# An attention and experts kernel on one core: preparation of a pair issued a unit later on ScalarE, hash factors on VectorE, the finish of a pair in smaller parts

## The chip, the cores and the metric

The kernel runs on one core of a Trainium2 chip. The metric is the device time of one execution in microseconds (us). TensorE (PE) multiplies matrices, VectorE (DVE), ScalarE (ACT) and GpSimd (POOL) work element by element, SyncE (SP) only issues transfers. Each engine takes its instructions in program order and waits on semaphores of the others.

## The reference

Three stages follow each other; the change touches the first alone, the attention. Queries and keys are hashed to 6 bits, and only those with the same hash attend to each other:

```python
q_bits = (np.einsum('bhsd,dk->bhsk', q, proj) > 0).astype(np.int64)
k_bits = (np.einsum('bhsd,dk->bhsk', k, proj) > 0).astype(np.int64)
q_bucket = np.sum(q_bits * powers, axis=-1)      # powers = 2 ** np.arange(6)
k_bucket = np.sum(k_bits * powers, axis=-1)
mask = q_bucket[:, :, :, None] == k_bucket[:, :, None, :]
scores = scale * np.matmul(q, k.transpose(0, 1, 3, 2))
scores = np.where(mask, scores, -1000000000.0)
scores = scores - np.max(scores, axis=-1, keepdims=True)
attn = np.exp(scores)
attn = attn / (np.sum(attn, axis=-1, keepdims=True) + 1e-09)
return np.matmul(attn, v)
```

There are 2 batches of 8 heads, 768 tokens, 64 numbers a head. The result, 1536 rows of 512, goes through gated products (`a * b @ w_out` with 1536 hidden columns) and then to one of 8 experts for each row.

## The kernel before

**Pairs and units.** Heads are taken in 8 pairs `i`; a pair fills the 128 partitions with two heads of 64. A head has six blocks of 128 queries, and a *unit* `u` is two of them, so a pair has six units and the attention has 48: `u = 6 i + r`. Tile `(u, t)` is block `t` (0 or 1) of unit `u`. The loop over `u` writes the whole order by hand; no scheduler moves anything.

**A tile's way.** `scores` (L170, L172, PE) multiplies queries and keys, and adds the product of the hash signs (`qf`, `kf`), which is zero for equal hashes and hugely negative otherwise; the buffer `st` in PSUM has two copies, so the scores of tile n+2 wait until the exponential has read tile n. `rowmax` (L177, DVE) takes the row maximum `nm`, `expo` (L183, ACT) the exponential `e` and its sum, `recip` (L187, DVE) and `normal` (L192 to L196, POOL) scale it, `turn` (L203, DVE) transposes it, and `pv` (L212, PE) multiplies it by `v`, four units behind: half a head in each unit with `u % 3` of 0 and 1. In the units with `u % 3 == 2` the `epilogue` (L230, ACT) copies the product out of the PSUM banks `pvb` and frees them.

**Preparing a pair.** Every sixth unit (1, 5, 11, 17, 23, 29, 35) `turned` transposes the raw queries and keys of a coming pair on PE into the banks `pvb` (L107), and ACT copies them to `k` and `q` (L121); four transfers on SP's queue make the swapped copies `ks` and `qs`, and `load` fetches the raw data of the pair after. Three units later (3, 8, 14, 20, 26, 32, 38) `signs` multiplies them by the hash projection (L145, L139, PE, into `pvb`), ACT takes the signs `sk` and `qf` (L150, L140), and two multiplications by `self.fac` make `kf` (L152, POOL; DVE for the first pair). These closures (`out`) run at the end of the same unit, behind `expo(u, 1)`.

**Finishing a pair.** `finish_add` (L234, POOL) adds the two halves of the product in three column groups of 256, `finish_high` (L238, ACT) casts the sum to `xh`, `finish_low` (L242, POOL) subtracts to get the rest `xl`. They run in the units with remainder 0 to 3 of the next but one pair.

**What else stands in the order.** `hook(u, at)` puts the conversion of the first weights of the gated products into the units, step by step (L396 to L424, on DVE, POOL and ACT), and in units 41, 44 and 47 the first gated products (L493, PE, into `pvb`) with their ACT copies L501 and L506.

Of the kernel before, what the change touches and what calls it, by code (L numbers as in the profile page):

```python
# [13 lines left out]
AF = mybir.ActivationFunctionType  # L14
ALU = mybir.AluOpType
# [6 lines left out]
def f32(ap):  # L22
    return ap.bitcast(F32)


class Kernel:
# [37 lines left out]
    def attention(self, xh, xl, pools, hook):  # L64
        nc = self.nc
        sb, ps_s, ps_pv = pools
        NB = self.proj.shape[1]
        S, D = self.S, self.D
        NC = S // 128
        pairs = [(b, hp) for b in range(self.B) for hp in range(self.H // 2)]  # L70

        NB32 = S // 32
        H2 = S // 2
# [6 lines left out]
        raw, Q, QS, K, KS, QF, KF, VR = {}, {}, {}, {}, {}, {}, {}, {}  # L80

        def load(i, qs=(nc.sync, nc.sync)):
            b, hp = pairs[i]
            t = raw[i] = sb.tile([128, 2, NC, 2, D], F32, tag="raw", name="raw", bufs=1)
            for j in range(2):
                for n, src in ((1, self.k), (0, self.q)):
                    qs[n].dma_start(out=t[:, n, :, j, :], in_=src[b, 2 * hp + j].rearrange("(p c) d -> p c d", c=NC))

        def load_v(h):
            (b, hp), j = pairs[h // 2], h % 2  # L90
            t = VR[h] = sb.tile([128, 4, NC * D], F32, tag="vr", name="vr", bufs=2)
            src = self.v[b, 2 * hp + j].rearrange("(a r c) d -> r a (c d)", a=4, c=NC)
            for a in range(4):
                nc.sync.dma_start(out=t[32 * a:32 * a + 32], in_=src)

        def halves(t):
            return t.rearrange("p (a b) -> p a b", a=2)
# [6 lines left out]
        def turned(i, n):  # L104
# [25 lines left out]

            return out

        def signs(i, n):
            p = pvb[:, 2 * n:2 * n + 2]
            lz = self.lz.rearrange("p a b c -> p (a b c)")
            if n == 0:
                QF[i] = sb.tile([128, S], BF16, tag="qf", name="qf", bufs=2)
                for x in range(2):
                    nc.tensor.matmul(p[:, x, :H2], lz, Q[i][:, x * H2:(x + 1) * H2], start=True, stop=True)  # L139
                return lambda: nc.scalar.activation(halves(QF[i]), p[:, :, :H2], AF.Sign, bias=self.bias, scale=2.0 ** 100)  # L140
            KF[i] = sb.tile([128, 2, H2], BF16, tag="kf", name="kf", bufs=2)
            sk = sb.tile([128, H2], BF16, tag="sk", name="sk", bufs=1)
            for x in range(2):
                r = slice(64 * x, 64 * x + 64)
                nc.tensor.matmul(  # L145
                    p[r, 0, :H2], lz[:, r], K[i][:, x * H2:(x + 1) * H2], start=True, stop=True, tile_position=(0, 64 * x)
                )

            def out(eng=nc.gpsimd):
                nc.scalar.activation(sk, p[:, 0, :H2], AF.Sign, bias=self.bias, scale=2.0 ** 100)  # L150
                for j in range(2):
                    eng.tensor_scalar(KF[i][:, j], sk, self.fac[:, j:j + 1], None, ALU.mult)  # L152

            return out

# [3 lines left out]
        def small(tag):  # L159
            return sb.tile([128, 2], F32, tag=tag, name=tag, bufs=4)  # L160

        def scores(u, t):
            i, j, g = units[u]
            c = 2 * g + t
            st = ST[u, t] = ps_s.tile([128, 2, 512], F32, tag="s", name="st")
            ql = slice(c * 128, (c + 1) * 128)
            rows = [slice(64 * n, 64 * n + 64) for n in range(2)]
            for n, d in enumerate(rows):
                q, k = (Q[i], K[i][:, n * H2:(n + 1) * H2]) if n == j else (QS[i], KS[i])
                nc.tensor.matmul(st[:, n, :H2], q[d, ql], k[d], start=True, stop=False, tile_position=(64 * n, 0))  # L170
            for n, d in enumerate(rows):
                nc.tensor.matmul(st[:, n, :H2], QF[i][d, ql], KF[i][d, j], start=False, stop=True, tile_position=(64 * n, 0))  # L172

        def rowmax(u, t):
            if t == 0:
                NM[u] = small("nm")
            nc.vector.tensor_reduce(NM[u][:, t:t + 1], ST[u, t][:, :, :H2], axis=AX.XY, op=ALU.max, negate=True)  # L177

        def expo(u, t):
            if t == 0:  # L180
                SU[u] = small("su")
            e = E[u, t] = sb.tile([128, 2, H2], F32, tag="e", name="e", bufs=6)
            nc.scalar.activation(e, ST.pop((u, t))[:, :, :H2], AF.Exp, bias=NM[u][:, t:t + 1], accum_out=SU[u][:, t:t + 1])  # L183
# [14 lines left out]
        def turn(u, t):  # L198
            i, j, g = units[u]
            h, c = 2 * i + j, 2 * g + t  # L200
            if c == 0:
                ET[h] = sb.tile([128, NB32, NC, 32], F32, tag="et", name="et", bufs=2)
            nc.vector.transpose(ET[h][:, :, c], E.pop((u, t)).rearrange("p a (b s) -> p (a b) s", s=32))  # L203
# [25 lines left out]
        def epilogue(h, n):  # L229
            nc.scalar.copy(place(h // 2, n, h % 2, every), product(n, every))  # L230

        def finish_add(i, col, rows=slice(0, 128), eng=nc.gpsimd):
            x, y = (t[rows, col] for t in XP[i])
            eng.tensor_tensor(x, x, y, ALU.add)  # L234

        def finish_high(i, col):
            b, hp = pairs[i]
            nc.scalar.copy(xh[b][:, hp, col], XP[i][0][:, col])  # L238

        def finish_low(i, col, eng=nc.gpsimd):  # L240
            b, hp = pairs[i]
            eng.tensor_tensor(xl[b][:, hp, col], XP[i][0][:, col], f32(xh[b][:, hp, col]), ALU.subtract)  # L242

        NU = len(units)
        cols = [slice(256 * g, 256 * g + 256) for g in range(3)]
# [13 lines left out]
        hook(-1, 0)  # L259
        load_v(0)  # L260
        load_v(1)
        signs(0, 1)(nc.vector)
        signs(0, 0)()
        scores(0, 0)

        for u in range(NU + 2):
            i, r = divmod(u, 6)
            s, w = u % 3, u - 2
            act, last, tr = u < NU, 0 <= u - 1 < NU, w >= 0
            done, fin = divmod(u - 11, 6) if u >= 11 else (-1, 0)  # L270
            preps, new = [], len(pairs)
            if u == 1 or s == 2 and r == 5:
                new = 1 if u == 1 else (u + 7) // 6
                kind = turned
            elif u == 3 or s == 2 and u > 2:
                new = 1 if u == 3 else i + 1
                kind = signs
            if act:
                rowmax(u, 0)
                scores(u, 1)  # L280
                expo(u, 0)
            if s == 2 and u >= 8:
                for n in range(2):
                    epilogue((u - 8) // 3, n)
            if u + 1 < NU:
                scores(u + 1, 0)
            if last:
                recip(u - 1)
                normal(u - 1)
            if tr:  # L290
                turn(w, 0)
            hook(u, 3)
            if act:
                rowmax(u, 1)
            if tr:
                turn(w, 1)
            if new < len(pairs):
                preps = [kind(new, x) for x in (1, 0)]
            elif s < 2 and u >= 6:
                pv((u - 6) // 3, range(12 * s, 12 * s + 12))  # L300
            hook(u, 0)
            if act:
                expo(u, 1)
            for prep in preps:
                prep(*((nc.scalar,) if kind is turned else ()))
            if preps and kind is turned and new + 1 < len(pairs):
                load(new + 1)
            if s == 1 and u >= 7 and (u - 1) // 3 < 2 * len(pairs):
                load_v((u - 1) // 3)
            hook(u, 1)  # L310
            if done == len(pairs) - 2:
                for g in range(3):
                    if fin == 1:
                        finish_add(done, cols[g])
                    if fin == 2:
                        finish_high(done, cols[g])
                        finish_low(done, cols[g])
            elif 0 <= done:
                if fin in (1, 2):
                    for g in ((0, 1), (2,))[fin - 1]:  # L320
                        finish_add(done, cols[g])
                if fin == 3:
                    finish_high(done, slice(0, S))
                if fin in (3, 4):
                    for g in ((0, 1), (2,))[fin - 3]:
                        finish_low(done, cols[g])
            hook(u, 4)
        end = len(pairs) - 1
        for n in range(2):
# [874 lines left out]
```

## Time and profile before

| what | us |
|---|---|
| median of three runs | 781.94 (781.47 to 782.32) |
| the profiled execution | 781.45 |
| its span, first to last instruction | 779.7 |
| PE busy in the span | 720.6 |
| POOL busy | 457.6 |
| DVE busy | 463.6 |
| ACT busy | 342.4 |
| attention, from the start to the last probability product | about 271 |

The rows below are read as follows. A row of the timeline has its start and its length, then engine, line, operation, written and read tiles with their shapes; in brackets the idle time of the engine ahead of it and who ended that. `x4` are four instructions merged. A row by windows has the stretch, its length, and the busy time of PE, PE's weight loads, DVE, ACT and POOL with their instruction counts, then the granted clock of PE as a share of 2.4 GHz, the busy share of the DMA engines and GB/s.

### The profile page before, as it was taken

The numbers are of one execution on the slowest core, as the hardware profiler recorded it, in microseconds if no ns is written. First come the engines' busy times: TensorE is split into PE (matmuls) and PEld (weight loads), VectorE is DVE, ScalarE is ACT, GpSimd is POOL, SyncE is SP. The second block draws the span as 40 slices with busy tenths as digits, with TensorE's granted clock in tenths as the row PEclk, the third lists the DMA queues.
The fourth block names the chain that finished last, engine by engine and source line by source line (L and its number), as shares of the span: only waits on it lengthen the run. The fifth ranks groups of instructions, "written<-read, shape, count | busy, mean of one in ns | idle before, by whom it ended". The sixth has DMA issues, their size and how long they took to land.

```text
span 779.7 us, 16454 instructions
## 1 busy us (share of the span) xinstructions
PE 720.6 (92%) x6832; PEld 599.8 (77%) x6832; DVE 463.6 (59%) x681; ACT 342.4 (44%) x597; POOL 457.6 (59%) x466
## 2 busy tenths in 40 slices
PE   6788888887887899999999999999999999999996
PEld 4345445454554789999999999999998898899995
DVE  3788787686777355364564555623754765556551
ACT  3566566566555434322212121223353755564651
POOL 0678879788787537356363562654441765565651
PEclk9999999999999999999999999999999999999999
DMA  6845273352313403113121130163252576675520
GB/s 151 166 114 117 67 178 77 80 146 55 95 43 89 131 1 110 53 59 105 31 78 55 55 108 3 51 216 107 87 160 91 175 232 235 213 247 202 211 76 22
DMA packets 67485, 87.62 MB, mean 112 GB/s; under 512 B 28739, under 2 KB 40003, under 8 KB 67408
## 3 DMA queue, kind: packets, MB, share of 16 engines
q1 hardware_dynamic: 63200, 78.81, 34.9%
q0 software_dynamic: 2560, 7.34, 2.5%
q8 instruction: 54, 0.88, 0.5%
q10 hardware_dynamic: 1648, 0.39, 0.3%
q14 instruction: 23, 0.19, 0.1%
HBM read 75.52 MB, written 7.34 MB: 106 GB/s over the span
## 4 chain that ended last, share of the span: by engine, by line
PE 78%; ACT 8%; DVE 5%; issue 4%; POOL 3%; DMA 1%; SPq 0%; POOLq 0%; ACTq 0%; DVEq 0%
PE ab L493 22%; PE yp L519 12%; PE op L836 10%; PE hp L786 9%; PE pv L212 8%; PE st L170 5%; ACT e L183 3%; DVE nm L177 2%; PE pv L139 2%; PE hr L804 2%; PE part L493 1%; PE lgp L602 1%; DVE et L203 1%; ACT co L230 1%; PE pv L493 1%
## 5 line engine op out<-in xcount | busy, mean ns | idle before, releaser
L493 PE MATMUL ab<-xh,w 128*128 128x384 f32 x704 | 185.7, 338 | 0.0
L493 PEld LDWEIGHTS ab<-xh,w 128*128 128x128 f32 x704 | 127.7, 188 | 0.8
L507 POOL TENSOR_TENSOR g<-a,g 128x384 fp32r<-128x384 f32 x48 | 54.8, 1141 | 114.5 <-ACT g L506 105.1
L183 ACT ACTIVATE e<-st,nm 128x768 f32<-128x768 f32 x96 | 86.5, 904 | 76.2 <-DVE nm L177 37.7
L493 PE MATMUL ab<-xl,w 128*128 128x384 f32 x352 | 118.3, 336 | 0.0
L177 DVE TENSOR_REDUCE nm<-st 128x1 f32<-128x768 f32 x96 | 90.5, 944 | 39.7 <-PE st L172 39.5
L742 POOL TENSOR_TENSOR w<-raw,w 128x1024 fp32r<-128x1024 f32 x36 | 88.1, 2450 | 36.8 <-ACT w L741 35.8
L170 PE MATMUL st<-ks,qs 64*128 64x384 f32 x192 | 86.3, 530 | 20.8 <-ACT e L183 20.8
L519 PE MATMUL yp<-w,g 128*128 128x512 f32 x432 | 103.4, 391 | 1.0 <-DVE a L505 0.7
L170 PE MATMUL st<-k,q 64*128 64x384 f32 x192 | 86.5, 531 | 14.8 <-ACT e L183 14.7
L196 POOL TENSOR_SCALAR e<-e,s,mc 128x768 f32<-128x768 f32 x96 | 96.1, 1008 | 5.3
L203 DVE STREAM_TRANSPOSE et<-e 128x768 f32<-128x768 f32 x96 | 92.5, 965 | 11.2 <-POOL e L196 9.3
L519 PEld LDWEIGHTS yp<-w,g 128*128 128x128 f32 x432 | 80.3, 188 | 16.7 <-DVE a L505 1.0
L836 PE MATMUL op<-w,hth 128*128 128x512 f32 x256 | 81.7, 400 | 0.0
L212 PE MATMUL pv<-et,vr 32*64 32x192 f32 x3072 | 79.4, 354 | 2.0 <-issue 1.5
L212 PEld LDWEIGHTS pv<-et,vr 32*64 32x64 f32 x3072 | 66.2, 145 | 19.5 <-issue 14.4
L786 PE MATMUL hp<-xgh,w 128*128 128x256 f32 x448 | 80.6, 281 | 0.0
L506 ACT CAST g<-a 128x384 fp32r<-128x384 f32 x48 | 24.8, 516 | 110.4 <-DVE a L505 110.4
L742 DVE TENSOR_TENSOR w<-raw,w 128x1024 fp32r<-128x1024 f32 x28 | 64.6, 2307 | 14.5 <-ACT w L741 14.5
L786 PEld LDWEIGHTS hp<-xgh,w 128*128 128x128 f32 x448 | 69.1, 188 | 0.3
L741 ACT CAST w<-raw 128x1024 fp32r<-128x1024 f32 x64 | 66.2, 1045 | 3.5 <-PE yp L519 3.5
L493 PEld LDWEIGHTS ab<-xl,w 128*128 128x128 f32 x352 | 66.2, 188 | 0.8
(190 smaller groups left out, 1183.8 us busy)
## 6 DMA issues: line engine op xcount, KB each, us to landing
raw<-in_moe_w_dram SPq DMA_DIRECT2D x32, 1024.0 KB, 5.3
vr<-in_v_dram SPq DMA_DIRECT2D x64, 192.0 KB, 3.9
raw<-in_moe_w_a_dram SPq DMA_DIRECT2D x5, 1024.0 KB, 5.0
raw<-in_moe_w_b_dram SPq DMA_DIRECT2D x5, 1024.0 KB, 5.3
raw<-in_moe_w_out_dram SPq DMA_DIRECT2D x5, 1024.0 KB, 5.0
raw<-in_k_dram SPq DMA_DIRECT2D x16, 192.0 KB, 4.9
qs<-q SPq DMA_DIRECT2D x16, 192.0 KB, 3.1
ybuf<-y SPq DMA_DIRECT2D x12, 256.0 KB, 6.3
```

The source lines that it names most:

```text
L170: nc.tensor.matmul(st[:, n, :H2], q[d, ql], k[d], start=True, stop=False, tile_position=(64 * n, 0))
L177: nc.vector.tensor_reduce(NM[u][:, t:t + 1], ST[u, t][:, :, :H2], axis=AX.XY, op=ALU.max, negate=True)
L183: nc.scalar.activation(e, ST.pop((u, t))[:, :, :H2], AF.Exp, bias=NM[u][:, t:t + 1], accum_out=SU[u][:, t:t + 1])
L196: nc.gpsimd.tensor_scalar(E[u, t], E[u, t], r[:, t:t + 1], c[:, t:t + 1], ALU.mult, ALU.add)
L203: nc.vector.transpose(ET[h][:, :, c], E.pop((u, t)).rearrange("p a (b s) -> p (a b) s", s=32))
L212: nc.tensor.matmul(pvb[m:m + 64, a, :NC * 32], v[d], et[d, n].rearrange("p c s -> p (c s)"), start=(n < 2), stop=(n >= NB32 - 2), tile_pos ...
L493: nc.tensor.matmul(p[:, :384], w[:, k, fs], x[:, k, cols], start=(k == 0 and n == 0), stop=(k == self.KD - 1 and n == 2),)
L519: nc.tensor.matmul(p, g[:, f, rows], w[:, f], start=(n == 0), stop=(n == 5))
L741: nc.scalar.copy(h, raw)
L742: eng.tensor_tensor(l, raw, f32(h), ALU.subtract)
L786: nc.tensor.matmul(p[:, :256], w[:, k, fs], x[:, k], start=(n == 0), stop=(n == 3 * self.KD - 1))
L836: nc.tensor.matmul(p, h[:, 2 * n + f, rows], w[:, f], start=(n == 0 and f == 0 and m == 0), stop=(n == 3 and f == 1 and m == 2),)
```

## The change

1. The closures of `turned` and `signs` are kept in `preps` and run in the next unit, behind that unit's first exponential `expo(u, 0)`; so do the copies' transfers and the `load` behind them. PE's part (transposes, sign products) stays where it was, now after `expo(u, 1)` in the text of the loop.
2. `expo(u, 1)` stands before `hook(u, 0)`, so before the ACT copies of the first gated products.
3. The two multiplications that make `kf` are put off into `later` and run on VectorE (`masks`), behind the second transposition of the unit in which ACT takes the signs.
4. The finish of a pair is a table: the cast `xh` in two parts of 512 and 256 columns, one unit apart from the additions and subtractions, over units with remainder 0 to 4. The last two pairs keep their own finish.

```diff
+        later = []
+        def masks():
+            for kf, sk in later:
+                for j in range(2):
+                    nc.vector.tensor_scalar(kf[:, j], sk, self.fac[:, j:j + 1], None, ALU.mult)
+            later.clear()
...
-            def out(eng=nc.gpsimd):
+            def out(*_):
                 nc.scalar.activation(sk, p[:, 0, :H2], AF.Sign, bias=self.bias, scale=2.0 ** 100)
-                for j in range(2):
-                    eng.tensor_scalar(KF[i][:, j], sk, self.fac[:, j:j + 1], None, ALU.mult)
+                later.append((KF[i], sk))
...
+        finish = (
+            (1, finish_add, (cols[0],)), (1, finish_add, (cols[1],)), (2, finish_add, (cols[2],)),
+            (2, finish_high, (slice(0, 512),)), (3, finish_low, (cols[0],)),
+            (4, finish_high, (cols[2],)), (4, finish_low, (cols[1],)), (5, finish_low, (cols[2],)),
+        )
...
             if act:
                 rowmax(u, 0)
                 scores(u, 1)
                 expo(u, 0)
+            for prep in preps:
+                prep(nc.scalar)
+            if preps and kind is turned and held + 1 < len(pairs):
+                load(held + 1)
+            preps = []
...
             if tr:
                 turn(w, 1)
+            masks()
+            if act:
+                expo(u, 1)
...
             if new < len(pairs):
-                preps = [kind(new, x) for x in (1, 0)]
+                preps, held = [kind(new, x) for x in (1, 0)], new
...
             hook(u, 0)
-            if act:
-                expo(u, 1)
-            for prep in preps:
-                prep(*((nc.scalar,) if kind is turned else ()))
-            if preps and kind is turned and new + 1 < len(pairs):
-                load(new + 1)
...
-                if fin == 3:
-                    finish_high(done, slice(0, S))
+                for start, step, args in finish:
+                    done, fin = divmod(u - 11 - start, 6)
+                    if fin == 0 and 0 <= done < len(pairs) - 2:
+                        step(done, *args)
```

What this does to the order is seen best at unit 26, where the signs of a pair are prepared. On ACT, from the epilogue of unit 26 on (`xp`, `co`), before:

```order
L230 COPY xp_2398<-pv_127 64x4x6x32
L230 COPY co_2399<-pv_127 64x4x6x32
L183 ACTIVATE e_2428,su_2395<-st_2390,nm_2388 128x768
L150 ACTIVATE sk_2422<-pv_127,bias_84 128x384
L140 ACTIVATE qf_2425<-pv_127,bias_84 128x768
L238 CAST xh0_98<-xp_1956 128x768
L183 ACTIVATE e_2445,su_2444<-st_2402,nm_2437 128x768
L183 ACTIVATE e_2513,su_2444<-st_2439,nm_2437 128x768
```

and after the change (line numbers are those of the changed file, the numbers of the tiles differ):

```order
L237 COPY xp_2402<-pv_127 64x4x6x32
L237 COPY co_2403<-pv_127 64x4x6x32
L190 ACTIVATE e_2425,su_2399<-st_2394,nm_2392 128x768
L190 ACTIVATE e_2443,su_2442<-st_2406,nm_2435 128x768
L158 ACTIVATE sk_2428<-pv_127,bias_84 128x384
L148 ACTIVATE qf_2431<-pv_127,bias_84 128x768
L190 ACTIVATE e_2467,su_2442<-st_2437,nm_2435 128x768
L245 CAST xh0_98<-xp_1959 128x256
```

The first exponential of unit 27 now stands ahead of the signs, the second behind them, and only the last part of the cast is left here, behind both.

On DVE, in unit 27 and at the start of unit 28, before:

```order
L177 TENSOR_REDUCE nm_2437<-st_2402 128x1
L187 RECIPROCAL r_2452<-su_2395 128x2
L203 STREAM_TRANSPOSE et_2417<-e_2312 128x24x32
L177 TENSOR_REDUCE nm_2437<-st_2439 128x1
L203 STREAM_TRANSPOSE et_2417<-e_2380 128x24x32
L177 TENSOR_REDUCE nm_2516<-st_2447 128x1
```

and after:

```order
L184 TENSOR_REDUCE nm_2435<-st_2406 128x1
L194 RECIPROCAL r_2452<-su_2399 128x2
L210 STREAM_TRANSPOSE et_2421<-e_2315 128x24x32
L184 TENSOR_REDUCE nm_2435<-st_2437 128x1
L210 STREAM_TRANSPOSE et_2421<-e_2335 128x24x32
L138 TENSOR_SCALAR kf_2427<-sk_2428,fac_86 128x384 x2
L184 TENSOR_REDUCE nm_2519<-st_2447 128x1
```

The two multiplications for `kf` come in between the second transposition of unit 27 and the first row maximum of unit 28. On POOL they stood between two units' `normal`, and are gone there. The order on SP's queue is the same before and after.

## Rows read from the trace of the kernel before

**Rows 1.** The page's slices of 19.5 us each: PE's busy tenths.

```profile
PE   6788888887887899999999999999999999999996
```

**Rows 2.** Windows from one pair's transposes to the next; the last ends at products.

```profile
38.22:67.52 29.30, 24.55 (x478) 14.66 (x477) 25.36 (x37) 18.13 (x34) 22.84 (x37) 1.00 0.36 86
67.52:98.77 31.25, 26.02 (x476) 15.76 (x477) 23.57 (x33) 19.22 (x36) 25.52 (x41) 0.95 0.48 117
98.77:129.49 30.72, 26.02 (x476) 15.76 (x476) 23.60 (x34) 19.23 (x36) 24.36 (x39) 0.94 0.48 115
129.49:160.50 31.01, 26.03 (x477) 15.61 (x477) 23.46 (x34) 19.32 (x36) 24.82 (x39) 0.94 0.41 94
160.50:190.85 30.35, 25.94 (x476) 15.80 (x476) 22.62 (x32) 18.63 (x34) 25.14 (x41) 0.94 0.40 97
190.85:221.67 30.82, 26.07 (x476) 16.11 (x476) 24.39 (x34) 18.18 (x34) 24.06 (x40) 0.94 0.38 98
```

**Rows 3.** Timeline of PE in units 24 to 27: scores and sign products.

```profile
133.53 0.59 PE L170 MATMUL st<-k,q 64*128 64x384 f32 x1 [1.48 <-ACT e L183]
...
143.70 0.87 PE L145 MATMUL pv<-k,lz 128*64 128x384 f32 x4 [0.41 <-ACT co L230]
...
145.99 0.59 PE L170 MATMUL st<-ks,qs 64*128 64x384 f32 x1
...
149.14 0.59 PE L170 MATMUL st<-ks,qs 64*128 64x384 f32 x1 [2.07 <-ACT e L183]
```

**Rows 4.** Windows of two `pv` runs and of unit 45's scores with their `pv`.

```profile
134.54:136.67 2.13, 2.13 (x98) 1.85 (x96) 1.91 (x3) 0.97 (x2) 1.77 (x6) 1.00 0.91 221
...
150.44:153.89 3.45, 3.45 (x98) 2.79 (x97) 2.01 (x3) 2.12 (x4) 3.08 (x7) 0.60 0.02 5
...
242.21:246.82 4.61, 4.61 (x103) 2.91 (x103) 3.56 (x6) 1.99 (x4) 4.17 (x8) 0.66 0.02 5
```

**Rows 5.** Timeline of ACT in units 23 to 27: copies, signs, cast, exponentials.

```profile
131.08 0.81 ACT L121 ACTIVATE k<-pv 128x768 f32<-128x768 f32 x1 [0.60 <-PE pv L107]
...
132.48 0.91 ACT L183 ACTIVATE e<-st,nm 128x768 f32<-128x768 f32 x1
...
142.85 0.80 ACT L230 COPY co<-pv 64x768 f32<-64x768 f32 x1
...
146.09 0.58 ACT L150 ACTIVATE sk<-pv,bias 128x384 bf16<-128x384 f32 x1 [1.43 <-PE pv L139]
...
147.36 0.83 ACT L238 CAST xh<-xp 128x768 fp32r<-128x768 f32 x1
148.08 0.91 ACT L183 ACTIVATE e<-st,nm 128x768 f32<-128x768 f32 x1
```

**Rows 6.** Timeline of DVE: the first row maxima of units 24 and 27.

```profile
130.32 0.95 DVE L177 TENSOR_REDUCE nm<-st 128x1 f32<-128x768 f32 x1
...
143.97 0.95 DVE L177 TENSOR_REDUCE nm<-st 128x1 f32<-128x768 f32 x1
```

**Rows 7.** Line L152: count, then ns min/median/max, first and last start (us).

```profile
L152 POOL TENSOR_SCALAR kf<-sk,fac x14: 1247/1253/1261, 32.3 to 208.8; 128x384 bf16<-128x384 bf16 x14
L152 DVE TENSOR_SCALAR kf<-sk,fac x2: 313/316/320, 11.8 to 12.0; 128x384 bf16<-128x384 bf16 x2
```

**Rows 8.** Timeline around unit 44: DVE's row maximum, ACT's cast, PE's scores.

```profile
238.90 0.95 DVE L177 TENSOR_REDUCE nm<-st 128x1 f32<-128x768 f32 x1
...
239.01 0.51 ACT L506 CAST g<-a 128x384 fp32r<-128x384 f32 x1 [3.12 <-DVE a L505]
...
240.59 0.59 PE L170 MATMUL st<-ks,qs 64*128 64x384 f32 x1 [2.28 <-ACT e L183]
```

**Rows 9.** Timeline: a conversion step on DVE twice, and POOL's `normal`.

```profile
38.81 2.12 POOL L196 TENSOR_SCALAR e<-e,s,mc 128x768 f32<-128x768 f32 x2
...
39.47 0.60 DVE L404 TENSOR_SCALAR r<-spare 128x512 int32<-128x512 uint32 x1
...
143.67 0.39 DVE L404 TENSOR_SCALAR r<-spare 128x512 int32<-128x512 uint32 x1
```

More of the change, by code (lines that the diff above doesn't have):

```diff
@@ L139, in signs @@
                     nc.tensor.matmul(p[:, x, :H2], lz, Q[i][:, x * H2:(x + 1) * H2], start=True, stop=True)
-                return lambda: nc.scalar.activation(halves(QF[i]), p[:, :, :H2], AF.Sign, bias=self.bias, scale=2.0 ** 100)
+                return lambda *_: nc.scalar.activation(halves(QF[i]), p[:, :, :H2], AF.Sign, bias=self.bias, scale=2.0 ** 100)
             KF[i] = sb.tile([128, 2, H2], BF16, tag="kf", name="kf", bufs=2)
@@ L261, in attention @@
         load_v(1)
-        signs(0, 1)(nc.vector)
+        signs(0, 1)()
+        masks()
         signs(0, 0)()
         scores(0, 0)
+        preps = []
[4 more added lines that the diff above has]
+        )
         for u in range(NU + 2):
@@ L270, in attention @@
             done, fin = divmod(u - 11, 6) if u >= 11 else (-1, 0)
[L271 to L277, printed above, removed]
+            new = len(pairs)
             if act:
@@ L281, in attention @@
                 expo(u, 0)
+            for prep in preps:
+                prep(nc.scalar)
+            if preps and kind is turned and held + 1 < len(pairs):
+                load(held + 1)
+            preps = []
             if s == 2 and u >= 8:
@@ L296, in attention @@
                 turn(w, 1)
+            masks()
+            if act:
+                expo(u, 1)
+            if u == 1 or s == 2 and r == 5:
+                new, kind = 1 if u == 1 else (u + 7) // 6, turned
+            elif u == 3 or s == 2 and u > 2:
+                new, kind = 1 if u == 3 else i + 1, signs
             if new < len(pairs):
-                preps = [kind(new, x) for x in (1, 0)]
+                preps, held = [kind(new, x) for x in (1, 0)], new
             elif s < 2 and u >= 6:
@@ L317, in attention @@
                         finish_low(done, cols[g])
[L318 to L321, printed above, removed]
-                if fin == 3:
-                    finish_high(done, slice(0, S))
-                if fin in (3, 4):
-                    for g in ((0, 1), (2,))[fin - 3]:
-                        finish_low(done, cols[g])
+            else:
+                for start, step, args in finish:
+                    done, fin = divmod(u - 11 - start, 6)
+                    if fin == 0 and 0 <= done < len(pairs) - 2:
+                        step(done, *args)
             hook(u, 4)
```

## Prediction, written before the changed kernel ran

> **What bounds the kernel now.** I read the page's slices first: from the fifteenth on (273 us), where the gated products have begun, PE is busy for 90% or more; before that, in the attention, mostly for 70 to 90% [rows 1]. So there is something to win in the attention alone. Then I cut the attention at the transposes of each pair [rows 2]: one pair of heads takes 29.3 to 31.3 us, and PE, the busiest engine, has work for 24.6 to 26.1 of it. So the change is worth what it takes out of the first 260 us, and each us there is a us of the whole, because PE works in order.
>
> The timeline of PE inside one pair shows where its 5 us of idling are. It runs gapless through the units with probability products, and stops at the unit that prepares another pair: 1.48 us before the scores at 133.53 and 2.07 us before those at 149.14, both times until an exponential on ACT [rows 3]. Why the exponential is late stands in ACT's timeline: the two copies k and q (131.08), or the two signs (146.09) and a cast of the finished pair (147.36), are queued ahead of it [rows 5]. Its row maximum had been ready long before: DVE starts the maximum for the 148.08 exponential at 143.97 [rows 6]. And the second stop costs more than itself: the 96 products after it take 3.45 us at a granted clock of 0.60, a mix of 1.2 and 2.4 GHz, where the same 96 took 2.13 us at 1.00 [rows 4].
>
> **The change, part by part: one pair walked through.** I take the pair of units 24 to 29 (129.49 to 160.50, 31.01 us), with the durations of the rows, and move what moves. A row maximum takes 0.95 and a hand-over of 0.1; from an exponential's start to the scores that need its buffer are 1.05 (132.48 to 133.53) [rows 3, 5].
>
> *Copies k and q a unit later.* DVE's maximum at 130.32 is untouched [rows 6], so the exponential starts at 130.32 + 1.05 = 131.37 instead of 132.48, the scores at 132.42 instead of 133.53. The copies follow: 131.37 + 0.89, then 1.40 for both (131.08 to 132.48), then 0.15 to the end and over to PE: 133.8. The probability products write the banks that q is read from, so they start there and not at 133.4 when the scores are through: a new wait of 0.4. Now they start at 134.54 [rows 4]. Gain 0.72. Everything up to the sign products (143.70) is PE after PE or hangs on it, and moves with it: 142.98.
>
> *Signs a unit later, the cast out of their way.* The sign products take 2.29 (143.70 to 145.99) and end at 145.27. The maximum of 143.97 comes at 143.25, its exponential at 144.3 instead of 148.08, and it frees the scores' buffer at 145.35. PE goes on without a stop: two scores tiles of 0.92, products at 147.1 instead of 150.44. Signs (0.48 and 0.9) run on ACT from 145.3 to 146.8, under these scores. Gain 3.34, of it 2.62 here. The cast cost 0.72 of the old chain (147.36 to 148.08); its two parts now stand behind exponentials of other units, where ACT waits 1 to 2 us for a maximum (0.62 and 0.41 estimated by columns; 0.2 more in sum, hidden).
>
> *Clock.* With no stop before them the products run at 1.00: 2.13 instead of 3.45, gain 1.32. They end at 149.23; now 153.89.
>
> *Masks on DVE.* Two of 0.316 (pitch 0.24, so 0.5 for both) [rows 7], behind the transposition of unit 27 and ahead of the maximum for tile (28,0). That maximum starts at 148.65, its exponential at 149.7, the scores of (29,0) at 150.75, where PE is free at 150.15: a new wait of 0.6. What had hidden such work, PE's stop, is gone. POOL loses 2.49 per pair, which ends the waits of DVE's transposition for it. From there: products to 153.9, the maximum of (29,0) at 152.25, exponential 153.3, behind it two epilogue copies of 0.8 (142.85) [rows 5], the next transposes at 155.85 instead of 160.50. **4.65 us for this pair.**
>
> *What the next pair pays.* DVE has become the engine that is a little late: the next pair's first maximum starts 1.5 us behind its transposes, where it was 0.83 (130.32 after 129.49), so q's copy frees the banks when it does now, and the 0.72 is lost. Repeating the walk with a lateness D, a pair takes 24.9 + D + the weight-conversion steps on DVE that stand right before the first maxima of units 26, 28 and 29 (0.3 to 0.7 us each; L404 is one of them [rows 9]); D is 0.96 plus the step before unit 30 less that before 29. Check: 24.9 + 0.83 + 0.6 for the one step before unit 26 = 26.3, as walked.
>
> *The sum.* Against the rows [rows 2]:
> - until 38.22: 0.3 (the exponential of unit 2 gains 1.6, then DVE's queue with masks and a conversion eats it);
> - 38.22 to 67.52, no cast yet and no clock lost: 27.3 for 29.30, gain 2.0;
> - 67.52 to 98.77: 26.65 for 31.25, gain 4.6; to 129.49: 27.2 for 30.72, gain 3.5; to 160.50, entered late: 27.1 for 31.01, gain 3.9; to 190.85: 26.5 for 30.35, gain 3.9;
> - 190.85 to 221.67: masks and two conversion steps collide before the first maximum of unit 40: 27.5 for 30.82, gain 3.3;
> - the last units, where the exponential is put ahead of the gated products' ACT work: in unit 41 about 0.5. In unit 44 a cast at 239.01 holds an exponential and with it the scores at 240.59, for 2.28 us [rows 8]. They now follow PE's products at 238.3; the next scores need the maximum of 238.90, so 241.0 instead of 242.21, and from there 3.0 instead of 4.61 us at clock 0.66 [rows 4]: 2.6. In unit 47 PE waits for ACT's copy of its own products either way: 0.
>
> Together 24.6. The profiled execution took 781.45 (781.94 is the median of three), so 756.8; against the median 757.3. I say **757**.
>
> **One rule weighed.** The rows show that a short DVE operation can be held: the same conversion step L404 took 0.39 at 143.67 and 0.60 at 39.47, where POOL was in an operation of 1.06 (two in 2.12) [rows 9]. The Trainium skill ("SBUF — State Buffer", Who interferes with whom) says why: a VectorE tensor_scalar in a two-port mode and any GpSimd operation take a shared port pair as an exclusive lock, and the second waits for the whole of the first. The masks are of that kind, so by it each could be held for most of a POOL operation, and the sum would come out up to 12 us worse. In my walk POOL has nothing to run between 146 and 148.7, so I take 0.5 for the two; the other end is the second rival.
>
> **Rivals.**
> 1. *The clock still falls.* PE keeps shorter stops (0.4, 0.6, two of 0.7 around the epilogue). If the granted clock stays at 0.6 in the products after the signs, 1.3 in each of five pairs is not gained: 763.5. Against it: stops of 1.5 us (133.53) left the products at 1.00. 0.10.
> 2. *DVE paces the pair.* Each mask is held by POOL for up to a whole operation, 1.06, and its followers with it: 2.1 per pair, six pairs, 12: 769 at the worst. For it: the 0.60 [rows 9], and DVE has little slack left (23.5 busy in a pair of 27 [rows 2], 24 with the masks). Against it: POOL idles there in the walk. 0.13.
> 3. *Given back in the dense stage*, if that were paced by its weight loads: then nothing changes, 781. Against it: PE's slices there are full as they are, and what starts earlier finds them the same [rows 1]. 0.02.
> 4. *Slower.* The signs are now queued on ACT behind an exponential that waits for DVE; the products wait for the signs, and all scores for the products. Before, the signs waited for PE alone. In the walk the maximum of (27,0) starts at 143.25; 0.55 later the signs end when PE wants the banks, and from there each us of DVE's lateness is a us of PE. From some 5 us of lateness in every pair the gain is gone; at 6 the kernel takes about 788. DVE would have to be held in front of that maximum by a transposition whose data POOL has not normalised. Against it: such waits are now of 1 to 2 us and follow POOL's masks, which leave. 0.04.
>
> **How the numbers follow.** Forecast 757 (752 to 762): 0.64. Rival 1: 0.10. Rival 2 (763 to 769): 0.13. Faster than 752: 0.05, if no pair is entered late (24.9 + 0.96 is the least, against PE's own 24.7). Something between 770 and 779, half the gain lost in a wait that I don't see: 0.02. Rivals 3 and 4: 0.02 and 0.04. 752 to 769 holds about 0.84. Within 0.2% is what a measurement of this kernel can tell from no change: 0.02; slower 0.04; faster 0.94.
>
> **What would show it.** Right: transposes of successive pairs 26.5 to 27.5 us apart; the exponential before the signs and not waiting for them; PE's clock 1.00 in the products after the signs; DVE busy about 24 of 27 in a pair, with the first maxima of units 24, 28 starting when DVE comes free, not when PE delivers; masks of 0.5 for two. Wrong: masks of 1 us and more; clock below 0.9 after the signs; products waiting over 0.5 us for the signs; a pair above 29 us.

## The result, and the profile after

The changed kernel takes **758.85 us** (median of four runs, 756.55 to 762.79) against 781.71 for the kernel before: ratio 0.9712, 95% interval 0.9671 to 0.9753. Forecast were 757.0 and a range of 752 to 769. The profiled execution took 759.07, with a span of 757.2; before 781.45 and 779.7. So the span lost 22.5 us where the sum said 24.6.

The page of the changed kernel: busy time, share and instructions of each engine, then PE's row of the 40 slices.

```profile
PE 712.5 (94%) x6832; PEld 594.9 (79%) x6832; DVE 466.6 (62%) x695; ACT 343.3 (45%) x603; POOL 437.8 (58%) x452
...
PE   6698888989887999999999999999999999999996
```

PE's slices of the attention, mostly 7 and 8 before [rows 1], are mostly 8 and 9 now, and the full ones begin with the fourteenth (246 us), not the fifteenth (273 us). The products of the last head start at 244.99, before at 266.90; what follows takes 512.2 us, before 512.8. So nothing of the gain was given back in the dense stage.

The windows between the transposes of successive pairs, as in [rows 2] (length, busy time of PE, its weight loads, DVE, ACT and POOL, granted clock, DMA share, GB/s):

```profile
38.25:65.47 27.22, 25.30 (x478) 15.69 (x477) 23.52 (x36) 17.48 (x33) 17.66 (x32) 0.96 0.41 96
65.47:94.42 28.95, 25.79 (x476) 15.35 (x476) 24.07 (x35) 19.35 (x36) 22.70 (x38) 0.94 0.50 115
94.42:121.69 27.27, 24.21 (x478) 14.59 (x477) 23.71 (x37) 19.39 (x36) 21.79 (x37) 1.00 0.58 133
121.69:148.69 27.00, 24.27 (x476) 14.59 (x477) 24.06 (x37) 19.28 (x36) 21.92 (x37) 1.00 0.51 111
148.69:175.27 26.58, 24.06 (x477) 14.59 (x477) 22.92 (x35) 18.84 (x35) 22.51 (x39) 1.00 0.50 113
175.27:202.41 27.14, 24.10 (x477) 14.63 (x477) 23.83 (x37) 18.36 (x35) 21.15 (x39) 1.00 0.43 107
```

Five of the six pairs are where the sum had them: it said 27.3 for the first, and 27.2, 27.1, 26.5 and 27.5 for the third to sixth. The second was to take 26.65 and takes 28.95. That one row is more than the whole difference between 24.6 and 22.5.

The pair that the prediction walked (units 24 to 29, now 121.69 to 148.69) in the timeline of PE (start, duration, what; in brackets the idle time before it and what ended it):

```profile
125.31 0.59 PE L177 MATMUL st<-k,q 64*128 64x384 f32 x1 [1.08 <-ACT e L190]
...
126.72 2.21 PE L219 MATMUL pv<-et,vr 32*64 32x192 f32 x96 [0.33 <-ACT q L121]
...
143.50 0.59 PE L177 MATMUL st<-ks,qs 64*128 64x384 f32 x1 [0.31 <-ACT e L190]
...
148.69 1.53 PE L107 MATMUL pv<-ident,raw 128*128 128x128 f32 x12 [0.16 <-ACT co L237]
```

The same stretch on ACT, the copies behind the exponential of (24,0) and the signs behind that of (27,0):

```profile
124.27 0.90 ACT L190 ACTIVATE e<-st,nm 128x768 f32<-128x768 f32 x1 [1.42 <-DVE r L194]
...
125.16 0.80 ACT L121 ACTIVATE k<-pv 128x768 f32<-128x768 f32 x1
125.85 0.81 ACT L121 ACTIVATE q<-pv 128x768 f32<-128x768 f32 x1
...
137.67 0.90 ACT L190 ACTIVATE e<-st,nm 128x768 f32<-128x768 f32 x1 [0.88 <-DVE r L194]
...
138.56 0.57 ACT L158 ACTIVATE sk<-pv,bias 128x384 bf16<-128x384 f32 x1
139.02 0.90 ACT L148 ACTIVATE qf<-pv,bias 128x768 bf16<-128x768 f32 x1
```

On DVE, the masks and the first maximum of unit 28:

```profile
140.99 0.51 DVE L138 TENSOR_SCALAR kf<-sk,fac 128x384 bf16<-128x384 bf16 x2
141.42 0.94 DVE L184 TENSOR_REDUCE nm<-st 128x1 f32<-128x768 f32 x1
```

And the window of the products behind these signs:

```profile
139.97:142.10 2.13, 2.13 (x98) 1.86 (x96) 2.13 (x5) 1.28 (x3) 1.24 (x4) 1.00 0.03 8
```

The exponential of unit 24 no longer stands behind k and q, that of unit 27 not behind the signs; the products behind the signs take 2.13 at a clock of 1.00, where a stop of 2.07 had left them 3.45 at 0.60 [rows 3, 4]. The new waits are there too: 0.33 for q's copy (0.4 was forecast), and 0.31 before the scores of (29,0), behind the masks (0.6 was forecast).

### The profile page after: what moved, and what is told of

Read it like the earlier page. It is cut to its first block, busy times and chain, and to the rows that moved or that the text cites. A ratio compares the mean times of both kernels' runs of the same rounds, so it can differ in the third digit from the quotient of the medians.

```text
span 757.2 us, 16448 instructions
## 1 busy us (share of the span) xinstructions
PE 712.5 (94%) x6832; PEld 594.9 (79%) x6832; DVE 466.6 (62%) x695; ACT 343.3 (45%) x603; POOL 437.8 (58%) x452
## 4 chain that ended last, share of the span: by engine, by line
PE 76%; DVE 10%; ACT 5%; issue 5%; POOL 2%; DMA 2%; SPq 0%; POOLq 0%; DVEq 0%; ACTq 0%
PE ab L503 24%; PE yp L529 13%; PE op L846 10%; PE hp L796 9%; PE pv L219 5%; DVE nm L184 4%; PE st L177 3%; DVE et L210 3%; ACT e L190 2%; PE hr L814 2%; PE part L503 1%; PE pv L147 1%; PE lgp L612 1%; POOL e L203 1%; PE xgt L773 1%
## 5 line engine op out<-in xcount | busy, mean ns | idle before, releaser
L517 POOL TENSOR_TENSOR g<-a,g 128x384 fp32r<-128x384 f32 x48 | 51.4, 1071 | 116.5 <-ACT g L516 106.9
L203 POOL TENSOR_SCALAR e<-e,s,mc 128x768 f32<-128x768 f32 x96 | 94.4, 991 | 5.4 <-POOL s L201 0.2
L177 PE MATMUL st<-ks,qs 64*128 64x384 f32 x192 | 86.1, 529 | 11.9 <-ACT e L190 11.9
L219 PEld LDWEIGHTS pv<-et,vr 32*64 32x64 f32 x3072 | 61.0, 134 | 20.7 <-issue 9.9
L219 PE MATMUL pv<-et,vr 32*64 32x192 f32 x3072 | 72.5, 332 | 4.3 <-issue 2.2
```

The lines of the kernel that those rows point to most:

```text
L203: nc.gpsimd.tensor_scalar(E[u, t], E[u, t], r[:, t:t + 1], c[:, t:t + 1], ALU.mult, ALU.add)
L219: nc.tensor.matmul(pvb[m:m + 64, a, :NC * 32], v[d], et[d, n].rearrange("p c s -> p (c s)"), start=(n < 2), stop=(n >= NB32 - 2), tile_pos ...
```

## The experiments

All were run beside the kernel before, whose median was 781.5, 781.1 and 781.0 us in the three sets; the changed kernel was run again in the second. Over all nine of its runs its median is 759.07, and the prices below are against that. With one part undone alone, the 95% interval of each of the five variants overlaps that of the changed kernel (that of the finish just barely), so a price of 1.6 to 3.9 us is a difference of medians, and it is the rows that show what a part does. Each profile is of a single execution.

**Signs back.** The sign activations are issued in their own unit again (behind its second exponential), the rest as changed.

```
             hook(u, 0)
+            if preps and kind is signs:
+                for prep in preps:
+                    prep(nc.scalar)
+                preps = []
```

> Only the two sign activations go back behind the second exponential of their own unit; copies, masks, finish parts and exponentials stay as changed. My theory (signs are what holds the exponential): the exponential of the next unit waits for signs again, PE stops 1.6 us before the scores of (28,0) and its equals, and in most pairs the clock falls behind it, 1.1 more: about 2.7 in each of six or seven pairs, so 770 to 776 us against 759 for the changed kernel. Rival (the cast in the signs' way was the cost, not the place of the signs): 759 to 763. Second rival (DVE paces the pair anyway): 759 to 762.

Measured: 762.75 us (761.86 to 762.81), ratio to before 0.9752 (0.9707 to 0.9798): 3.7 more, not 11 to 17. Its fourth pair on ACT and PE:

```profile
140.45 0.58 ACT L158 ACTIVATE sk<-pv,bias 128x384 bf16<-128x384 f32 x1 [1.43 <-PE pv L147]
...
140.93 0.89 ACT L148 ACTIVATE qf<-pv,bias 128x768 bf16<-128x768 f32 x1
...
141.72 0.90 ACT L190 ACTIVATE e<-st,nm 128x768 f32<-128x768 f32 x1
...
142.76 0.59 PE L177 MATMUL st<-ks,qs 64*128 64x384 f32 x1 [1.33 <-ACT e L190]
...
143.77 2.21 PE L219 MATMUL pv<-et,vr 32*64 32x192 f32 x96
```

The queue is as expected: signs, then the exponential, then the scores after a stop. But the stop is 1.33 and leaves the clock up, in six pairs of six; and while PE stands there the masks cost nothing, so that the stops before (29,0) are gone. What is left is 0.6 us a pair on average: beside the second profile of the changed kernel (below), in which the clock stayed up in these pairs, the second pair is 0.35 shorter, the third to fifth are 1.0 to 1.2 longer, and the sixth is as long. The time lies in the first rival's range; but the rows show that the signs do hold the exponential, so the rival has the number and not the reason. The expectation had priced a longer stop, a fall of the clock behind it, and no cover for the masks.

**Finish back.** Only the finish goes back to its old units, with one cast of 768 columns.

```
-            else:
-                for start, step, args in finish:
...
+            elif 0 <= done:
...
+                if fin == 3:
+                    finish_high(done, slice(0, S))
+                if fin in (3, 4):
+                    for g in ((0, 1), (2,))[fin - 3]:
+                        finish_low(done, cols[g])
```

> Only the finish of a pair goes back to its old units, with the cast of all 768 columns in one. My theory: with the signs a unit later the cast (0.83) falls into ACT's idle time before the exponential of (27,0) and costs nothing there: 757 to 761 us, though unit 44 may lose up to 2 us by its cast. Rival (the cast in one piece delays an exponential of each pair by 0.7 and the clock falls): 765 to 772 us.

Measured: 764.3 us (764.0 to 766.5), ratio 0.9785 (0.9737 to 0.9833): 5.2 more, outside the range of either theory. The cast holds the exponential behind it up by 0.1 to 0.3, in the third pair by 0.5. In the pairs PE does not stop for that, as I had it, and the stop of unit 44 grows from 1.68 to 1.88; it is POOL that pays. POOL and DVE of the fourth pair:

```profile
141.99 1.41 POOL L249 TENSOR_TENSOR xl<-xp,xh 128x256 fp32r<-128x256 f32 x2 [1.92 <-ACT xh L245]
...
144.42 2.03 POOL L203 TENSOR_SCALAR e<-e,s,mc 128x768 f32<-128x768 f32 x2
...
145.39 1.17 DVE L138 TENSOR_SCALAR kf<-sk,fac 128x384 bf16<-128x384 bf16 x2
...
146.48 0.94 DVE L184 TENSOR_REDUCE nm<-st 128x1 f32<-128x768 f32 x1
```

The two subtractions (141.99) wait for the whole cast and stand ahead of the normalisation, which then runs (144.42) when the masks come. These take 1.17 in the place of 0.51, in four of the last five pairs, and the first maximum behind them is late by as much: the stop before (29,0) is 1.02, where it was 0.31. The six stops of this kind add to 9.2 us here and to 5.7 in the changed kernel, and behind one of them (1.90) the clock fell. So I read most of the 5 us not as the shorter cast but as a POOL that is in short operations or idle when the masks run. No run has the cast in one piece and the subtractions in their new places, so this division stays argued from the rows.

**Both back.** Signs and finish together, so that the cast stands between the signs and the exponential as before.

> The signs go back behind the second exponential of their own unit, and the finish of a pair goes back to its old units with one cast of 768 columns, which then stands between the signs and the exponential again; the rest as changed. My theory (signs and cast are one queue: 1.3 of stop from the signs, 0.7 from the cast, and only the two together make PE stop long enough, 2.07, for the clock to fall): 771 to 777 us, 3 to 8 more than the two prices added. Rival (each has its price by itself, 3.9 and 5.4 over the changed kernel): 768.

Measured: 771.02 us (769.62 to 774.34), ratio 0.9874 (0.9843 to 0.9904): 11.9 more, where the two prices add to 8.9. Cast and exponential on ACT, then PE:

```profile
145.84 0.83 ACT L245 CAST xh<-xp 128x768 fp32r<-128x768 f32 x1
...
146.56 0.91 ACT L190 ACTIVATE e<-st,nm 128x768 f32<-128x768 f32 x1
...
147.62 0.59 PE L177 MATMUL st<-ks,qs 64*128 64x384 f32 x1 [2.07 <-ACT e L190]
...
148.68 3.60 PE L219 MATMUL pv<-et,vr 32*64 32x192 f32 x88
```

Here is the 2.07 of before [rows 3], 1.33 from the signs and 0.74 from the cast, and the products behind it are slow again. It stands so in five pairs, and behind three of them the clock fell (in the profile of before behind all five). Theory and number hold, at the lower edge: neither part alone brings PE to a stop of 2.07 at this place.

**The others back.** The counterpart: only signs and finish as changed; copies, exponentials and masks as before (the three small diffs below together).

> Only the signs a unit later and the finish in smaller parts are kept; the copies of k and q, the exponentials and the masks (on POOL) stand as in the kernel before. My theory (signs and cast carry about half of the gain, 11 us as both_back shows from the other side, and the other parts hide one another little): 765 to 770 us. Rival (the walk as predicted, in which signs, cast and clock were 4.7 of each pair and the rest 0): 757 to 760. Second rival (nothing is gained without the others): 777 or more.

Measured: 771.5 us (771.09 to 772.14), ratio 0.9868 (0.9843 to 0.9893). Signs and finish alone are worth 9.5 us, the other three parts alone 10.1 (both back), all five 22. That is 1.5 beyond my range, and far from the rival that gave signs and cast the whole of a pair's gain (757 to 760). In its profile the stop of 1.47 before (25,0) is there in every pair, unit 41 stops for 1.46 and 0.95 and unit 44 for 2.28.

**The three small parts.** The copies of k and q back in their own unit:

```
             hook(u, 0)
+            if preps and kind is turned:
+                for prep in preps:
+                    prep(nc.scalar)
+                if held + 1 < len(pairs):
+                    load(held + 1)
+                preps = []
```

> Only the copies of k and q go back behind the second exponential of their own unit. My theory: what they gain on PE's stop before (25,0) is given back in the products' wait for the banks and in DVE's lateness, so 0 to 0.4 per pair: 758 to 762 us. Rival (the copies cost what their rows show, a stop of 1.5 us per pair): 765 to 770.

Measured: 760.65 us (760.01 to 761.96), ratio 0.9735 (0.9688 to 0.9781), 1.6 more. The stop before (25,0) is 1.47 in each pair, where it was up to 1.31, and the 0.33 for q's copy is gone: little, as walked. Part of the price is hidden in the second pair: there the masks take 0.63 and the stop behind them is 0.83, in the changed kernel 1.65 and 1.85.

The second exponential back behind the gated products:

```
-            if act:
-                expo(u, 1)
...
             hook(u, 0)
+            if act:
+                expo(u, 1)
```

> Only the second exponential of a unit goes back behind the gated products of units 41, 44 and 47 and their ACT work; everything else as changed. My theory: in unit 44 the exponential waits for the products (208 to 211.5 where the copy of g ends), and PE's next scores with it, 1 to 2.3 us; in unit 41 1 to 2: 761 to 764 us against 759 to 760. Rival (only the cast was in the way in unit 44): 758 to 760.

Measured: 761.54 us (760.83 to 763.68), ratio 0.9748 (0.9722 to 0.9775), 2.5 more. The stop in unit 41 grows from 0.52 to 1.46, that in unit 44 from 1.68 to 2.28.

The masks back on POOL, behind the sign activation:

```
-                later.append((KF[i], sk))
+                for j in range(2):
+                    nc.gpsimd.tensor_scalar(KF[i][:, j], sk, ...)
```

> Only the masks go back to POOL, behind the sign activation; everything else as changed. My theory: DVE gets 0.5 us per pair back, and the stops of PE before (29,0) (0.3 to 1.0, in the second pair 1.85 and a fall of the clock) go, 3 to 5 us in all; POOL gets 2.5 per pair, and DVE's transposition behind it comes 0.3 to 0.5 later: 755 to 760 us, so the move to DVE brought nothing by itself. Rival (POOL's masks hold the normalisation and with it DVE): 1 to 2.5 per pair, 765 to 775 us.

Measured: 762.95 us (760.51 to 767.29), ratio 0.9777 (0.9722 to 0.9831), 3.9 more, beyond my range. Its profile is that of its fastest run and shows 1.4 of the 3.9. The pairs changed little in it: from the transposes that end the first pair to the gated products of unit 41, five pairs take 136.4 us (66.61 to 202.99). In the changed kernel they take 136.9 (65.47 to 202.41) with one fall of the clock, and 135.3 (69.73 to 205.05) in its second profile without one. The larger difference is in unit 41, which takes 15.3 us up to the products of unit 44, in the changed kernel 13.4. There a conversion step of DVE waits for one of POOL in front of a first maximum:

```profile
204.78 1.28 POOL L418 TENSOR_TENSOR late<-late,r 128x512 int32<-128x512 int32 x1
...
206.09 0.69 DVE L429 SCALAR_TENSOR_TENSOR late<-late 128x512 f32<-128x512 f32 x1 [3.17 <-POOL late L418]
...
206.71 0.95 DVE L185 TENSOR_REDUCE nm<-st 128x1 f32<-128x768 f32 x1
...
208.81 0.59 PE L178 MATMUL st<-k,q 64*128 64x384 f32 x1 [2.46 <-ACT e L191]
```

In the changed kernel POOL does that step at 202.29, DVE waits 0.65 for it, and PE stops for 0.52. So the move bought POOL's time, not DVE's. The masks are POOL's only added work. In the last pair they take 2.49 (from 191.68), ahead of a normalisation that starts at 195.31, and from there POOL runs almost without a pause up to the late step. In the changed kernel the same normalisation starts at 190.02, and POOL then waits 2.93 us for DVE.

**The changed kernel again**, for its spread:

> The changed kernel as it is, beside its variants. My theory (its spread of 6 us comes from stops of PE of 1.7 us and more, behind which the granted clock sometimes falls): 756 to 763 us again, the longer runs with the lower mean clock. Rival (the spread is of one chip or one hour): within 1 us.

Measured: 759.89 us (757.82 to 760.68), inside my range, with a spread of 2.9, so the rival's 1 us does not hold. Of the nine runs the two fastest had mean clocks of 0.994 and 0.993, the slowest (762.79) 0.984. But the stops are not all of it. The two profiles of this kernel are 3.1 us apart already at the transposes that begin the first pair: 38.25, at a mean clock of 0.98 from 7 us on, and 41.39, at 0.87. In the second profile the second pair has the same late maximum and a stop of 1.83 (1.85 there), but the clock stayed up. The pair, and the stretch from the stop on:

```profile
69.73:97.21 27.48, 24.20 (x476) 14.58 (x476) 24.11 (x36) 19.35 (x36) 22.70 (x38) 1.00 0.57 129
92.07:96.80 4.73, 4.73 (x114) 3.11 (x114) 3.79 (x6) 3.21 (x6) 4.37 (x8) 1.00 0.07 17
```

So the same pair takes 27.48 at full clock and 28.95 without. Of the 2.30 that were missing there, 1.47 are the clock; the remaining 0.83 I put down to the late maximum (without it, in masks late below, this pair takes 26.01).

**Masks late.** The masks stand on DVE behind the first maximum of units 5, 11, ..., 29, 35, those with the next transposes, and no longer ahead of a first maximum.

```
+            if r == 5:
+                masks()
             if u + 1 < NU:
                 scores(u + 1, 0)
...
                 turn(w, 1)
-            masks()
```

> The changed kernel with the masks moved on DVE from ahead of the first maximum of units 4, 10, 16, ... to behind the first maximum of the unit after, where DVE waits up to 2.3 us for POOL. My theory (the masks are what stops PE before the scores of (29,0) and its equals, and once the clock falls with it): the stops of 0.96, 1.85, 0.82, 0.31, 0.36 and 1.43 become 0 to 0.9, 4 us in all with the clock: 753 to 757 us. Rival (DVE's whole work paces the pair, the place of the masks does not matter): 758 to 762.

Measured: 755.11 us (752.07 to 756.83), ratio 0.9651 (0.962 to 0.9682): 4.0 less, and the stop in the second pair is 0.26 in the place of 1.85. DVE there:

```profile
88.04 0.92 DVE L184 TENSOR_REDUCE nm<-st 128x1 f32<-128x768 f32 x1
88.88 1.01 DVE L138 TENSOR_SCALAR kf<-sk,fac 128x384 bf16<-128x384 bf16 x2
```

The masks take 7.0 us in all, in the changed kernel 5.4, since POOL is in an operation more often when they come, and still the kernel is faster. What counted was what stands behind them. The rival falls with the time (758 to 762 were expected by it). In the fifth pair of this profile the clock falls behind a stop of 1.39; the changed kernel stops there too (1.31) and kept its clock.

**Steps late.** In addition DVE's conversion steps at the end of a unit go behind the first maximum of the next.

```
             if act:
                 rowmax(u, 0)
+            hook(u - 1, 4)
+            if act:
                 scores(u, 1)
...
-            hook(u, 4)
```

> As masks_late, and the weight-conversion steps of DVE at the end of a unit (0.4 to 0.85 us each) moved behind the first maximum of the next unit too. My theory (every DVE operation right ahead of a first maximum is paid by PE in the scores that wait for it): 1 to 3 us less than masks_late, 751 to 755 us, and the stop before the scores of (25,0) and its equals goes from 1.1 to about 0.5. Rival (DVE's whole work paces the pair): no less than masks_late, or 759.

Measured: 750.73 us (748.9 to 752.34), ratio 0.9607 (0.9581 to 0.9634): 4.4 less than masks late, where 1 to 3 were expected, and 8.3 less than the changed kernel. The interval does not overlap that of the changed kernel, and that of masks late just barely. The stop before the scores of (25,0) is 0.28 (about 0.5 was expected). Windows of its second to fourth pair:

```profile
65.14:91.14 26.00, 24.21 (x476) 14.68 (x476) 24.68 (x37) 19.27 (x36) 22.68 (x38) 1.00 0.60 137
91.14:116.67 25.53, 24.04 (x477) 14.68 (x477) 23.76 (x36) 19.40 (x36) 22.53 (x39) 1.00 0.60 137
116.67:142.20 25.53, 24.04 (x477) 14.67 (x477) 23.89 (x35) 19.50 (x36) 21.81 (x39) 1.00 0.55 118
```

DVE has as much work as in the changed kernel, but these pairs need only 25.5 to 26.0 us (the fifth 26.4, the sixth 26.0). So DVE's whole work did not pace the pair; the place of its short operations did. The rival falls. Two masks with POOL beside them, in the same kernel:

```profile
139.14 1.28 POOL L419 TENSOR_TENSOR spare<-spare,r 128x512 int32<-128x512 int32 x1
...
139.35 1.88 DVE L138 TENSOR_SCALAR kf<-sk,fac 128x384 bf16<-128x384 bf16 x2
```

**Fill late.** In the order of DVE and ACT the gated products' work of units 41 and 44 goes behind the next unit's first maximum and exponential; PE's own order stays.

```
-            if act:
+            if u - 1 in (41, 44):
+                expo(u, 0)
+                hook(u - 1, 0)
+                scores(u, 1)
+            elif act:
                 scores(u, 1)
                 expo(u, 0)
...
-            hook(u, 0)
+            if u not in (41, 44):
+                hook(u, 0)
```

> As steps_late, and the gated products of units 41 and 44 put, in the order of DVE and ACT, behind the next unit's first maximum and exponential (PE's own order stays). My theory (the stop of 1.68 in unit 44 comes from the first maximum of unit 45, which stands on DVE behind the product that waits for PE): that stop and the 0.46 of unit 41 go, 1.5 to 2.1 us less than steps_late, 748 to 749.5 us. Rival (the exponential of unit 45 is late for another reason): 750 to 751.

Measured: **748.11 us** (747.66 to 749.61), ratio 0.9574 (0.9548 to 0.96): 2.6 less than steps late, the fastest of all. The two intervals overlap, but the rows show the stop go. First steps late, in which the first maximum of unit 45 stands behind a product that waits for PE:

```profile
210.44 0.56 DVE L517 TENSOR_TENSOR a<-pv,a 128x384 f32<-128x384 f32 x1 [1.93 <-PE pv L505]
...
210.91 0.95 DVE L184 TENSOR_REDUCE nm<-st 128x1 f32<-128x768 f32 x1
...
213.02 0.59 PE L177 MATMUL st<-ks,qs 64*128 64x384 f32 x1 [1.68 <-ACT e L190]
```

Then fill late, with that maximum (209.28) ahead of the product:

```profile
209.28 0.92 DVE L184 TENSOR_REDUCE nm<-st 128x1 f32<-128x768 f32 x1
211.09 0.56 DVE L522 TENSOR_TENSOR a<-pv,a 128x384 f32<-128x384 f32 x1 [0.89 <-PE pv L510]
```

The stop of 1.68 is gone there; one of 0.36 stands a unit later. From the gated products of unit 44 to those of unit 47 are 13.22 us, in steps late 14.80.

## Why the prediction was right, point by point

- *The place of the gain.* Right: from the transposes of the first pair to the products of the last head 206.74 us, before 228.68.
- *Copies a unit later.* Right in kind and size: 0.33 for q's copy where 0.4 stood, and the 0.72 lost in later pairs since DVE is late there. It starts the maximum 1.54 behind the transposes (123.23 after 121.69), and 1.5 was forecast.
- *Signs and cast.* Right as a walk with every part in place (3.9 for the fourth pair, 4.01 measured), wrong as a list of prices: the signs alone are worth 3.7 us in all, and the cast behind signs issued late holds ACT up by 0.1 to 0.5. Each part hides the next.
- *Clock.* Right where it was put: 1.00 in the products behind the signs, in five of five windows. Not foreseen: in the profiled run it falls behind other stops (87.80 and 220.87).
- *Last units.* 3.1 forecast, 2.65 measured, and in this profile that is near by luck. Unit 41 (up to the products of unit 44) gained 0.86 where 0.5 stood, unit 44 0.98 where 2.6 stood, and unit 47 0.81 where 0 stood. The scores of unit 44 moved up as walked, but a stop of 1.68 is left, and behind it the clock was at 0.64. In unit 47 a fall of the clock of before (0.68 behind 254.35) did not come. In the second profile, with the clock up behind the same stop of 1.68, unit 44 gained 2.63: there the term holds.
- *Until 38.22.* 0.3 forecast, nothing measured; from there to 40.80 PE ran at a clock of 0.58. In the profiles of the variants the first such transposes start anywhere between 37.8 and 41.4.
- *Rivals.* Nothing was given back in the dense stage, and the products never waited for the signs. The second rival's mechanism came in one pair, and with it a fall of the clock, though not in the products behind the signs, where the first rival had put it. That pair is the term that failed. The second pair also shows one of the prediction's own signs of being wrong (masks of 1 us and more); in the five others the two masks take 0.50 to 0.63.
- *Chances.* Those of the forecast and the first two rivals, which make up 752 to 769, add to 0.87; the prediction says about 0.84.

**The step that failed** is the 4.6 of the second pair; 2.30 came. The prediction's words are: "In my walk POOL has nothing to run between 146 and 148.7, so I take 0.5 for the two". In the fourth pair that holds (0.51). In the second POOL was still normalising:

```profile
82.69 1.96 POOL L203 TENSOR_SCALAR e<-e,s,mc 128x768 f32<-128x768 f32 x2
84.60 0.74 POOL L249 TENSOR_TENSOR xl<-xp,xh 128x256 fp32r<-128x256 f32 x1
...
83.81 1.65 DVE L138 TENSOR_SCALAR kf<-sk,fac 128x384 bf16<-128x384 bf16 x2
...
85.39 0.41 DVE L406 TENSOR_SCALAR spare<-spare 128x512 int32<-128x512 int32 x1
...
85.72 0.94 DVE L184 TENSOR_REDUCE nm<-st 128x1 f32<-128x768 f32 x1
...
87.80 0.68 PE L177 MATMUL st<-ks,qs 64*128 64x384 f32 x1 [1.85 <-ACT e L190]
...
89.39 3.24 PE L219 MATMUL pv<-et,vr 32*64 32x192 f32 x96
```

The window from the stop on:

```profile
87.80:92.56 4.76, 4.76 (x102) 3.02 (x103) 2.56 (x4) 1.98 (x4) 4.26 (x8) 0.64 0.00 0
```

The masks take 1.65, a conversion step of 0.41 comes behind them, and only then the maximum; PE stands for 1.85, and the clock falls to 0.64 in what follows. That is the second rival's mechanism once (0.83) and, behind the stop that it made, a fall of the clock once (1.47). Two masks take 0.51 with POOL idle or in operations of 0.24. Here they take 1.65: the first (0.96) ends behind the second of two normalisations (1.96 for both), the second (0.78) behind the subtraction of 0.74. In steps late they take 1.88, the first (1.18) beside an addition of 1.28. The rule of the Trainium skill that the prediction weighed ("SBUF — State Buffer", Who interferes with whom), a lock for the length of the other's operation, agrees with these rows.

## What to carry to other kernels

Where one engine paces and another feeds it by a short chain (a maximum, its exponential, a buffer that comes free), look at every instruction that stands directly ahead of the chain's first link on its engine, however short: moving masks and conversion steps, most of them under 1 us, behind it gave 8.3 us here (759.07 to 750.73), with no work taken away. An operation may well be put where it takes longer, if nobody waits behind it. And parts that share one queue have no prices of their own: two that cost 3.7 and 5.2 when undone apart cost 11.9 together.

## What the runs showed of the hardware

How often the granted clock falls goes with how long PE stood, but not with that alone. I counted the stops of PE in these thirteen profiles, from 45 us to the last attention products, that an instruction of ACT ended. Behind stops of 1.0 to 1.5 us the clock was under 0.95, as a mean over the 3.5 us that I took behind each, in 2 of 51 cases, behind 1.5 to 2.0 us in 3 of 16, behind more than 2 us in 18 of 26. The same stop of 1.68 us in unit 44 left it up in six profiles and lowered it in one. The levels are 1.2 and 2.4 GHz, so that a mean of 0.64 over 4.76 us is a mix. The spread of a kernel's runs does not simply follow their number: the four or five runs of the masks back, with five such stops in the profile, lie 6.8 us apart and those of fill late, with one, 2.0, but those of the signs back, with eight, 0.95 and those of the others back, with twelve, 1.05. What decides in a single case stays open.
